# Semaphore waits on TensorE moved to earlier products, smaller fill products, another order at both ends of the kernel

## The chip, the cores and the metric

The kernel runs on one core of a Trainium2 chip. A core has five engines with a queue each: PE (TensorE, with its weight loads listed apart as PEld), DVE (VectorE), ACT (ScalarE), POOL (GpSimd) and SP (SyncE, which issues most of the DMAs here). They work side by side and wait for each other by semaphores. The metric is the time of the device for one execution, in microseconds (us); all times below are in us where nothing else stands.

## What is computed

Retention attention over 8 batches, 8 heads, 576 positions and heads of 64, then a mixture of small adapters on the result, in which each token takes 2 of 8 experts:

```python
scores = scale * np.matmul(q, k.transpose(0, 1, 3, 2))
Dmat = np.where(rel >= 0, gamma[:, None, None] ** rel[None, :, :], 0.0)
ret = np.matmul(scores * Dmat[None], v)              # B, H, S, D
x = ret.transpose(0, 2, 1, 3).reshape(B * S, H * D)  # 4608 x 512
logits = x @ w_gate
topk = np.argpartition(-logits, K, axis=1)[:, :K]    # K = 2
...                                                  # w: softmax of the two logits
delta[mask] += w[mask, k, None] * ((x[mask] @ A[e]) @ B[e])
return x + delta
```

## The kernel before, in words

**Units and rounds.** The 576 positions are cut into four chunks of 128 and a short one of 64. A unit is one chunk of two batches (or the short chunk of four); there are 16 full and 2 short units, `seq` lists them, and all four batch pairs of one chunk come before the next chunk. The short ones are units 14 and 17. The attention is done chunk by chunk with a running state `P` per batch pair, so the scores are needed only inside a chunk; units 0 to 3 (chunk 0) have no earlier state.

The loop over `t` from 2 to 17 is a software pipeline. Round `t` works on three units: `u` = t, `p1` = t-1 and `p2` = t-2. The program's order on every engine is that of the code, written out by hand (`tc.manual_schedule()`), and each engine runs its own queue in that order. In a full round PE does, in this order:

- `stage_B(p2)`: 8 transposes of x into the output bank (po), so that x is added to the adapters' result
- `stage_R0(p1)`: 16 products of masked scores with v, the same-half part, which finish px
- `stage_S(u)`: 32 products of q and k, the scores (ps)
- `stage_X(p2)`: two transposes of the routed z (pzt); `stage_Z(p1)`: 8 products of x with A and the gate (pz); `stage_Y(p2)`: 4 products with B (po)
- `stage_Q(u)`: 16 products of q with the state P (px); left out for chunk 0
- `stage_U(u)`: 16 products of v and k, the update of the state (pu)
- `stage_R1(u)`: 16 products of masked scores with v, the other part (px)
- `stage_T` for q and then k of unit t+1: 8 transposes each (pt_q, pt_k), 64 rows at a time

A product of float32 operands is two weight loads and two matmuls on PE, so the 32 products of the scores are listed as 64.

**The other engines.** DVE multiplies the transposed q by its decay out of PSUM (qT, two halves of a unit, line 254), masks the scores (rt, four per unit, line 306), adds to the state (pn, line 342) and does the routing: `route` finds the two best logits (max, ns), has ACT take the sigmoid (sg), and scales z (cm, zc). ACT copies the transposed k out of PSUM (kT, line 263): two copies per unit, r = 0 with the first 64 positions of every head pair and r = 1 with the second 64. In the scores, the products of the loop variable `late` = 0 read the first half of kT and those with `late` = 1 the second; the fifth product of `stage_S` is the first with `late` = 1. ACT also copies x (xT), the outputs (osb) and zT. POOL scales v by the decay (two halves, `scale_v`), swaps the halves of the second batch (vs) and decays the state. SP issues the loads of unit t+4 in round t, and the stores.

**Waits.** An instruction of an engine carries one wait on one semaphore. Where it has to wait for two, a record of its own stands ahead of it in the engine's queue and carries the other wait (EVENT_SEMAPHORE in the trace). In the kernel before a full round has five such records on PE: ahead of the first product of `stage_U` (which waits for DVE's masks, as its bank held scores, and for POOL's v), ahead of the first and the second transpose of q (its DMA, and DVE's routing, which read the bank before), ahead of the first transpose of k (its DMA and DVE), and ahead of the first product of `stage_S` (qT from DVE, kT from ACT).

**PSUM.** There are eight banks, k0 to k7, handed out by hand: `bank(i, ...)`. `a`, `c`, `d`, `e` in the loop name pairs of banks; `c` and `d` change places every round.

**Ahead of the loop.** PE first runs fill products on a constant tile `ones` while nothing else is there, then `pa`, which makes the table of decays `aqp`; units 0 and 1 run by hand-written order, with the making of the adapter weights AW (pl) between them.

**After the loop.** The last full unit (p1 = 16) and the last short one (u = 17) are routed, multiplied by B and stored.

Of the kernel before, what the change touches and what calls it, by code (L numbers as in the profile page):

```python
# [18 lines left out]
def kernel(  # L19
# [124 lines left out]
    seq.append((NFULL, 1))  # L144
    NU = len(seq)
    nat = {}


    def alloc_nat(i):
# [7 lines left out]
    def load_part(i, w):  # L157
        c, y = seq[i]
        src, tl = (q, k, v)[w], nat[i][w]
        for s in range(2):  # L160
            if c < NFULL:
                nc.sync.dma_start(  # L162
                    out=tl[:, s * H : s * H + H, :],
                    in_=src[2 * y + s, :, 128 * c : 128 * c + 128, :].rearrange(
                        "h j d -> j h d"
                    ),
                )
            else:
                b0, s0 = QUAD * y + 2 * s, 128 * NFULL
                nc.sync.dma_start(  # L170
                    out=tl[64 * s : 64 * s + LH, :, :],
                    in_=src[b0 : b0 + 2, :, s0 : s0 + LH, :].rearrange("b h j d -> j (b h) d"),
                )
# [17 lines left out]
        mybir.DependencyClass.Sync, mybir.DependencyReason.DATA  # L191
    )

    class Unit:
        pass

# [12 lines left out]
    flat = lambda t_: t_.rearrange("p a b d -> p (a b d)")  # L209

    def scale_b(u, b, eng):
        eng.tensor_tensor(  # L212
            out=u.v[:, b * H : b * H + H, :],
            in0=u.v[:, b * H : b * H + H, :],
            in1=(gv if u.full else gvh).unsqueeze(2).broadcast_to((128, H, Dh)),
            op=ALU.mult,
        )

    def swap_v(u):

# [11 lines left out]
    def stage_T(u, nm, bk, halves=False):  # L232
        src = u.q if nm == "q" else u.k
        dst = wk.tile([128, HP, 2, 128], FP32, tag=nm + "T", name=nm + "T", bufs=4)
        ps = [bank(bk[r], [128, HP, 2, 64], f"pt_{nm}") for r in range(2)]
        for b in range(2):
            for hp in range(HP):
                for r in range(2):
                    sl = slice(64 * r, 64 * r + 64)
                    nc.tensor.matmul(  # L240
                        ps[r][:, hp, b, :],
                        lhsT=src[sl, b * H + 2 * hp : b * H + 2 * hp + 2, :],
                        rhs=id64[sl, :],
                        is_transpose=True,
                        start=True,
                        stop=True,
                    )

        n = HP // 2 if halves else HP
        for hp in range(0, HP, n):  # L250
            for r in range(2):
                i_, hs = slice(64 * r, 64 * r + 64), slice(hp, hp + n)
                if nm == "q":
                    nc.vector.tensor_tensor(  # L254
                        out=dst[:, hs, :, i_],
                        in0=ps[r][:, hs],
                        in1=aqp[:, hs, i_ if u.full else slice(0, 64)]
                        .unsqueeze(2)
                        .broadcast_to((128, n, 2, 64)),
                        op=ALU.mult,  # L260
                    )
                else:
                    nc.scalar.copy(out=dst[:, hs, :, i_], in_=ps[r][:, hs])  # L263
        setattr(u, nm + "T", dst)

    def mm(o, l, r, start, stop):
# [33 lines left out]
    def mask(u, gs=(0, 1)):  # L300
        if 0 in gs:
            u.rt = [[None, None], [None, None]]
        for g in gs:
            for ho in range(2):
                r = wk.tile([128, 2, 3, 64], FP32, tag=f"rt{ho}", name=f"rt{ho}", bufs=4)
                nc.vector.tensor_tensor(  # L306
                    out=r.rearrange("p a s i -> p a (s i)"),
                    in0=u.ps[ho][g].rearrange("p a s i -> p a (s i)"),
                    in1=tri3.rearrange("p s i -> p (s i)").unsqueeze(1).broadcast_to((128, 2, 192)),
                    op=ALU.mult,  # L310
                )
                u.rt[ho][g] = r

    def stage_Q(u, bk):
        u.px = [bank(bk[b], [128, HP, 128], f"px{b}") for b in range(2)]
        if u.c == 0:
            return
        for hp in range(HP):
            for b in range(2):
                for ho in range(2):  # L320
                    mm(
                        u.px[b][half(ho ^ b), hp, :],
                        P[u.bp][half(ho), hp, b, :],
                        u.qT[half(ho), hp, b, :],
                        hp == 0,
                        False,
                    )

    def stage_U(u, bk):
        u.pu = bank(bk, [128, HP, 2, Dh], "pu")  # L330
# [13 lines left out]
            )  # L344
        nc.gpsimd.tensor_tensor(out=flat(P[u.bp]), in0=flat(pn), in1=flat(gdec), op=ALU.mult)  # L345

    def stage_R1(u):
        for b in range(2):
            for hp in range(HP):
                for ho in range(2):  # L350
                    mm(
                        u.px[b][half(ho ^ b), hp, 64:128],
                        u.vb[b][:, 2 * hp + ho, :],
                        u.rt[ho][hp // 2][:, hp % 2, 1 + b, :],
                        u.c == 0 and hp == 0,
                        True,
                    )

    def stage_R0(u, seen=None):
        first = True
        seen = seen or u.sum
        for hp in range(HP):
            for b in range(2):
                for ho in range(2):
# [7 lines left out]
                    if first:  # L374
                        tc.add_manual_dep(m.ins, seen.ins.name, done, reason="rows")
                        first = False


    def short_S(u, bk):
# [105 lines left out]

    def route(u, ss=(0, 1), away=False):
        if 0 in ss:
# [4 lines left out]
            u.zc = mo.tile([128, 2, ER], FP16, tag="zc", name="zc", bufs=4)  # L494
        m8, ns, sg, cm = u.rw
        z = {s: u.pz[s] for s in ss}
        if away:

            z[1] = mo.tile([128, ER + E], FP32, tag="z", name="z", bufs=1)
            nc.vector.tensor_copy(out=z[1], in_=u.pz[1])  # L500
        lg = {s: z[s][:, ER : ER + E] for s in ss}

        def best(s):
            nc.vector.max(out=m8[:, s, :], in_=lg[s])  # L504
            nc.vector.scalar_tensor_tensor(  # L505
                out=ns[:, s, :], in0=m8[:, s, 0:1], scalar=-1.0, in1=m8[:, s, 1:2],
                op0=ALU.mult, op1=ALU.subtract,
            )
            nc.scalar.activation(  # L509
                out=sg[:, s, :], in_=lg[s], func=AFT.Sigmoid, scale=2.0, bias=ns[:, s, :]  # L510
            )

        def times(s):
            nc.vector.scalar_tensor_tensor(
                out=cm[:, s, :], in0=lg[s], scalar=m8[:, s, 1:2], in1=sg[:, s, :],
                op0=ALU.is_ge, op1=ALU.mult,
            )
            nc.vector.tensor_tensor(
                out=u.zc[:, s, :].rearrange("p (e r) -> p e r", e=E),
                in0=z[s][:, 0:ER].rearrange("p (e r) -> p e r", e=E),  # L520
                in1=cm[:, s, :].unsqueeze(2).broadcast_to((128, E, R)),
                op=ALU.mult,
            )

        for s in ss:
            best(s)
        for s in ss:
            times(s)


    def stage_X(u, bk, cols=True):
# [69 lines left out]
    def filler(bk, n, cols):  # L601
        for _ in range(n):
            mm(
                bank(bk, [128, 4, 128], "fill")[:, 0 : cols // 128],
                ones[:, 0:128],
                ones[:, 0:128].unsqueeze(1).broadcast_to((128, cols // 128, 128)),
                True,
                True,
            )

    filler(7, 2, 512)
    pa = bank(6, [128, HP, 128], "pa")
    for hp in range(HP):
        mm(pa[:, hp, :], g8[:, 128 * (1 + hp) : 128 * (2 + hp)], g8[:, 0:128], hp == 0, True)
    nc.scalar.copy(out=aqp[:, 0 : HP // 2], in_=pa[:, 0 : HP // 2])
    nc.vector.tensor_copy(out=aqp[:, HP // 2 :], in_=pa[:, HP // 2 :])
    filler(7, 1, 256)
    for b in range(2):
        affine(tri3[half(b), 0 : 3 - b : 2 - b, :], [[0, 2], [1, 64]], -1, ALU.is_ge)
        nc.gpsimd.memset(tri3[half(b), 1 + b, :], 1.0)  # L620
# [22 lines left out]
    u0, u1 = get(0), get(1)  # L643
    stage_T(u0, "q", (2, 3), True)
    stage_T(u0, "k", (0, 1), True)
    filler(7, 1, 256)
    scale_b(u0, 0, nc.vector)
    scale_b(u0, 1, nc.gpsimd)
    swap_v(u0)
# [24 lines left out]
    stage_Z(u0, (2, 3))  # L674
    scale_v(u1)
    nc.gpsimd.dma_start(out=Bcat, in_=moe_B.rearrange("e r d -> (e r) d"))
    route(u0)
    stage_S(u1, (6, 7, 0, 1))
    mask(u1)
    stage_Q(u1, (6, 7))  # L680
    stage_U(u1, 4)
    state(u1)
    stage_R1(u1)
    transposes(2, (4, 5), (0, 1))

# [7 lines left out]
    for t in range(2, NU):  # L693
# [7 lines left out]
            stage_Z(p2, (None, c[0]), [1])  # L701
            route(p2, [1], True)
        if p1.full:
            stage_R0(p1)
            copy_x(p1)
            if u.full:
                stage_S(u, c + a)
# [15 lines left out]
        if u.full:  # L723
# [10 lines left out]
            else:  # L734
                stage_Q(u, c)
                stage_U(u, a[0])
                state(u)
                stage_R1(u)
        else:
            short_R(u)  # L740
            copy_x(u, True)
# [9 lines left out]
    stage_B(p1, a)  # L751
    stage_X(p1, d0, False)
    stage_Z(u, (d1, c[1]), [0])
    route(u, [0])
    stage_Z(u, (d1, c[1]), [1])
    stage_Y(p1)
    route(u, [1])
    evac(p1, [0])
    zT = mo.tile([128, 2, 128], FP16, tag="zT", name="zT")

    def last_X(s):
# [3 lines left out]
        )  # L765
        nc.scalar.copy(out=zT[:, s, :], in_=pzt)

    last_X(0)
    last_B(u, e + (c[0], d0))
    last_X(1)  # L770
    evac(p1, [1], nc.vector.tensor_copy)
    store(p1)
# [1 line left out]
    for s in range(2):  # L774
        for cc in range(2):
            mm(u.po[s][cc], zT[:, s, :], bv[:, :, cc ^ s, :], False, True)
        for cc in range(2):
# [3 lines left out]
            else:  # L781
                nc.scalar.copy(out=o, in_=u.po[s][cc])
        b0 = 4 * u.x + 2 * s
        nc.sync.dma_start(
            out=out3[b0 : b0 + 2, 128 * u.c : 128 * u.c + LH, :].rearrange("n t d -> t n d"),
            in_=u.osb[:, s].rearrange("p a o d -> p (a o d)"),
        )
# [31 lines left out]
```

## Time and profile before

| | us |
|---|---|
| median of 6 runs | 185.41 (182.98 to 187.21) |
| profiled execution, whole time | 182.98 |
| its span, first to last instruction | 181.3 |
| granted TensorE clock | 0.993 of full |
| DMA moved | 38.85 MB, 214 GB/s in the mean |

The profiled execution is one execution; its view of instructions is what the steps below are read from. Its page, cut down:

```profile
PE   7999899999999999999999999999998979999970
DVE  1546764745565756565555556565654663655560
ACT  3345154545353535353535344434341722335540
POOL 7470962918271809090908181727277007215000
DMA  6998999998999999998979998999999989511035
...
L254 DVE TENSOR_TENSOR qT<-pt_q,aqp 128x512 f32<-128x512 f32 (+1 forms) x38 | 23.3, 657 | 15.0 <-PE pt_q L240 15.0
L263 ACT COPY kT<-pt_k 128x512 f32<-128x512 f32 (+1 forms) x38 | 19.5, 568 | 31.4 <-PE pt_k L240 31.3
```

The first five rows cut the span into 40 equal slices of 4.5 us; a digit is the busy share of the slice in tenths. PE is full in nearly all of them and the DMA engines in most; the others are half busy. The last two rows are groups of instructions: line, engine, operation, what is written from what, shapes and count, then busy time and the mean of one in ns, then the idle time of the engine just ahead of them and what ended it. Both groups wait for PE: the queues of DVE and ACT are empty when the transposes come.

### The profile page before, as it was taken

The numbers are of one execution on the slowest core, as the hardware profiler recorded it, in microseconds if no ns is written. First come the engines' busy times: TensorE is split into PE (matmuls) and PEld (weight loads), VectorE is DVE, ScalarE is ACT, GpSimd is POOL, SyncE is SP. The second block draws the span as 40 slices with busy tenths as digits, with TensorE's granted clock in tenths as the row PEclk, the third lists the DMA queues.
The fourth block names the chain that finished last, engine by engine and source line by source line (L and its number), as shares of the span: only waits on it lengthen the run. The fifth ranks groups of instructions, "written<-read, shape, count | busy, mean of one in ns | idle before, by whom it ended". The sixth has DMA issues, their size and how long they took to land.

```text
span 181.3 us, 10252 instructions
## 1 busy us (share of the span) xinstructions
PE 171.8 (95%) x4636; PEld 155.2 (86%) x4636; DVE 100.6 (56%) x275; ACT 76.3 (42%) x177; POOL 81.4 (45%) x102
## 2 busy tenths in 40 slices
PE   7999899999999999999999999999998979999970
PEld 2789799999898989899999999999897969989850
DVE  1546764745565756565555556565654663655560
ACT  3345154545353535353535344434341722335540
POOL 7470962918271809090908181727277007215000
PEclk9999999999999999999999999999999999999997
DMA  6998999998999999998979998999999989511035
GB/s 139 263 221 201 233 230 229 227 232 199 248 260 222 254 217 264 218 259 187 277 174 289 245 264 185 247 214 247 218 264 222 276 185 281 205 56 66 4 124 225
DMA packets 119035, 38.85 MB, mean 214 GB/s; under 512 B 114248, under 2 KB 114376, under 8 KB 118992
## 3 DMA queue, kind: packets, MB, share of 16 engines
q1 hardware_dynamic: 118688, 38.04, 85.2%
q8 instruction: 36, 0.59, 1.3%
q0 software_dynamic: 144, 0.13, 0.6%
q10 hardware_dynamic: 160, 0.03, 0.1%
q14 instruction: 7, 0.06, 0.1%
HBM read 28.88 MB, written 9.44 MB: 211 GB/s over the span
## 4 chain that ended last, share of the span: by engine, by line
PE 87%; DVE 3%; DMA 2%; SPq 2%; issue 1%; POOL 1%; ACT 0%; ACTq 0%
PE px L267 23%; PE pz L267 19%; PE ps L267 11%; PE pu L267 9%; PE pt_q L240 6%; PE po L548 5%; PE pt_k L240 5%; PE po L267 4%; DMA v<-in_v_dram 2%; SPq L162 2%; PE pzt L536 2%; PE ps_s L267 1%; DVE rt L306 1%; DVE ns L505 1%; PE pl L267 1%
## 5 line engine op out<-in xcount | busy, mean ns | idle before, releaser
L345 POOL TENSOR_TENSOR P<-pn,gdec 128x512 f32<-128x512 f32 x16 | 20.4, 1275 | 72.9 <-DVE pn L342 54.0
L212 POOL TENSOR_TENSOR v<-v,pack 128x512 f32<-128x512 f32 x35 | 35.8, 1044 | 8.5 <-DMA v<-in_v_dram 8.5
L306 DVE TENSOR_TENSOR rt<-ps,tri 128x384 f32<-128x384 f32 x64 | 31.3, 550 | 14.5 <-PE ps L267 14.4
L267 PE MATMUL pz<-AW,xT 128*128 128x136 f32 x288 | 37.9, 284 | 0.7 <-issue 0.7
L267 PEld LDWEIGHTS pz<-AW,xT 128*128 128x128 f32 x288 | 34.7, 190 | 1.2 <-issue 0.9
L263 ACT COPY kT<-pt_k 128x512 f32<-128x512 f32 (+1 forms) x38 | 19.5, 568 | 31.4 <-PE pt_k L240 31.3
L254 DVE TENSOR_TENSOR qT<-pt_q,aqp 128x512 f32<-128x512 f32 (+1 forms) x38 | 23.3, 657 | 15.0 <-PE pt_q L240 15.0
L509 ACT ACTIVATE sg<-pz,ns 128x8 f32<-128x8 f32 x35 | 9.4, 268 | 42.0 <-PE po L267 26.5
L267 PE MATMUL ps<-qT,kT 64*64 64x128 f32 (+1 forms) x1024 | 25.9, 247 | 0.9 <-issue 0.9
L267 PEld LDWEIGHTS ps<-qT,kT 64*64 64x64 f32 x1024 | 23.8, 133 | 1.9 <-issue 1.1
L267 PE MATMUL px<-rt,v 64*64 64x64 f32 (+1 forms) x512 | 21.8, 224 | 0.2
L267 PE MATMUL px<-rt,vs 64*64 64x64 f32 (+1 forms) x512 | 21.2, 223 | 0.0
L223 POOL COPY vs<-v 64x512 f32<-64x512 f32 x32 | 19.5, 609 | 1.7
L267 PE MATMUL pu<-v,k 128*64 128x64 f32 x512 | 18.9, 225 | 0.7 <-POOL v L212 0.7
L267 PEld LDWEIGHTS px<-rt,v 64*64 64x64 f32 (+1 forms) x512 | 17.9, 136 | 1.9 <-DVE rt L306 0.4
L267 PEld LDWEIGHTS pu<-v,k 128*64 128x64 f32 x512 | 16.4, 137 | 3.6 <-issue 2.3
L450 ACT COPY xT<-px 128x512 f32<-128x512 f32 x33 | 18.0, 591 | 2.7 <-PE px L267 1.8
L504 DVE MAX8 m<-pz 128x8 f32<-128x8 f32 x35 | 6.1, 174 | 22.7 <-PE pz L267 16.5
L573 ACT COPY osb<-po 128x512 f32<-128x512 f32 x33 | 17.7, 588 | 0.0
L267 PEld LDWEIGHTS px<-rt,vs 64*64 64x64 f32 (+1 forms) x512 | 17.6, 136 | 0.0
L267 PE MATMUL px<-qT,P 64*64 64x128 f32 (+1 forms) x512 | 15.6, 262 | 0.0
L267 PEld LDWEIGHTS px<-qT,P 64*64 64x64 f32 x512 | 12.4, 133 | 2.6 <-DVE m L504 2.3
(68 smaller groups left out, 179.3 us busy)
## 6 DMA issues: line engine op xcount, KB each, us to landing
q<-in_q_dram SPq DMA_DIRECT2D x36, 256.0 KB, 5.0
k<-in_k_dram SPq DMA_DIRECT2D x36, 256.0 KB, 4.6
v<-in_v_dram SPq DMA_DIRECT2D x36, 256.0 KB, 4.6
out_dram<-osb SPq DMA_DIRECT2D x36, 256.0 KB, 4.3
A<-in_moe_A_dram SPq DMA_DIRECT2D x1, 256.0 KB, 4.1
Bcat<-in_moe_B_dram POOLq DMA_DIRECT2D x1, 128.0 KB, 3.7
g<-c_g ACTq DMA_DIRECT2D x1, 20.0 KB
pack<-c_rest ACTq DMA_DIRECT2D x1, 10.0 KB, 2.9
```

What stands on the lines that cost most here:

```text
L212: eng.tensor_tensor(out=u.v[:, b * H : b * H + H, :], in0=u.v[:, b * H : b * H + H, :], in1=(gv if u.full else gvh).unsqueeze(2).broadcast ...
L223: nc.gpsimd.tensor_copy(out=vs[half(1 - r)], in_=u.v[half(r), H : 2 * H, :])
L240: nc.tensor.matmul(ps[r][:, hp, b, :], lhsT=src[sl, b * H + 2 * hp : b * H + 2 * hp + 2, :], rhs=id64[sl, :], is_transpose=True, start=Tru ...
L254: nc.vector.tensor_tensor(out=dst[:, hs, :, i_], in0=ps[r][:, hs], in1=aqp[:, hs, i_ if u.full else slice(0, 64)] .unsqueeze(2) .broadcast ...
L263: nc.scalar.copy(out=dst[:, hs, :, i_], in_=ps[r][:, hs])
L267: return nc.tensor.matmul(o, lhsT=l, rhs=r, start=start, stop=stop, skip_group_check=True)
L306: nc.vector.tensor_tensor(out=r.rearrange("p a s i -> p a (s i)"), in0=u.ps[ho][g].rearrange("p a s i -> p a (s i)"), in1=tri3.rearrange(" ...
L345: nc.gpsimd.tensor_tensor(out=flat(P[u.bp]), in0=flat(pn), in1=flat(gdec), op=ALU.mult)
L450: nc.scalar.copy(out=o, in_=u.px[s])
L509: nc.scalar.activation(out=sg[:, s, :], in_=lg[s], func=AFT.Sigmoid, scale=2.0, bias=ns[:, s, :])
L548: nc.tensor.matmul(po[cc][:, s, dt, :], lhsT=u.xT[s][sl, dt, :], rhs=id64[sl, :], is_transpose=True, start=(dt == 0 and s == 0), stop=Fals ...
L573: copy(out=bass.AP(o.tensor, o.offset, ap), in_=u.po[cc])
```

## The change

It has five parts.

1. A helper `behind(m, other)` adds to a product a wait for an instruction of another engine. It is used at the end of three stages: the last two products of `stage_Q` wait for v's first scaling and for the last mask; the last three of `stage_R1` (in the loop, except where the unit ahead is short) wait for the routing of p1 and for the first loads of the next unit's q and k; the last one of `stage_R0` waits for the second kT copy of the unit whose scores come next. The products that follow then have one wait left each.
2. `route` is cut into `best` and `times`, so that the two can be issued apart.
3. The fill products at the start read 512 columns of `ones` in place of 128 repeated ones; one of 64 columns is added, two of 256 columns are taken out, and 13 products of 64 x 64 are put in ahead of unit 0's scores. The table `aqp` is made by one ACT copy in place of one half by ACT and one by DVE.
4. `route(u0)` is issued after `state(u1)` in place of ahead of `stage_S(u1)`.
5. At the end, both `best` are issued ahead of both `times`; the last transposes of x (`last_B`) come ahead of `last_X(0)`; the second of the last two stores is issued on ACT's queue in place of SP's.

The diff, without the lines that only keep the handles:

```diff
+    def behind(m, other):
+        tc.add_manual_dep(m.ins, other.ins.name, done, reason="split")
...
@@ def scale_b
+        if b == 0:
+            u.scaled = m
...
@@ def stage_T
-                    nc.scalar.copy(out=dst[:, hs, :, i_], in_=ps[r][:, hs])
+                    u.kT_made = nc.scalar.copy(out=dst[:, hs, :, i_], in_=ps[r][:, hs])
...
@@ def mask
-                nc.vector.tensor_tensor(
+                u.masked[g] = nc.vector.tensor_tensor(
...
@@ def stage_Q
+                    if hp == HP - 1 and b == 1:
+                        behind(m, (u.scaled, u.masked[1])[ho])
...
-    def stage_R1(u):
+    def stage_R1(u, ahead=()):
         for b in range(2):
             for hp in range(HP):
                 for ho in range(2):
...
+                    last = (b * HP + hp) * 2 + ho - 4 * HP + len(ahead)
+                    if last >= 0:
+                        behind(m, ahead[last])
...
-    def stage_R0(u, seen=None):
+    def stage_R0(u, nxt=None, seen=None):
...
+        if nxt:
+            behind(m, nxt.kT_made)
...
-    def route(u, ss=(0, 1), away=False):
+    def best(u, s, away=False):
...
+    def times(u, s):
...
+        u.routed = nc.vector.tensor_tensor(
...
+    def route(u, ss=(0, 1), away=False):
         for s in ss:
-            best(s)
+            best(u, s, away)
         for s in ss:
-            times(s)
+            times(u, s)
...
@@ def filler
-                bank(bk, [128, 4, 128], "fill")[:, 0 : cols // 128],
+                bank(bk, [128, 512], "fill")[:, 0:cols],
                 ones[:, 0:128],
-                ones[:, 0:128].unsqueeze(1).broadcast_to((128, cols // 128, 128)),
+                ones[:, 0:cols],
...
     filler(7, 2, 512)
+    filler(7, 1, 64)
...
-    nc.scalar.copy(out=aqp[:, 0 : HP // 2], in_=pa[:, 0 : HP // 2])
-    nc.vector.tensor_copy(out=aqp[:, HP // 2 :], in_=pa[:, HP // 2 :])
-    filler(7, 1, 256)
+    nc.scalar.copy(out=aqp, in_=pa)
...
     stage_T(u0, "k", (0, 1), True)
-    filler(7, 1, 256)
+
+    fb = [bank(i, [128, 64], "fill") for i in (7, 6)]
+    for i in range(13):
+        r, x = i % 2, i // 2 % 2
+        mm(fb[r ^ x][half(x), :], id64[half(r), :], id64[half(r), :], True, True)
...
-    route(u0)
     stage_S(u1, (6, 7, 0, 1))
     mask(u1)
     stage_Q(u1, (6, 7))
     stage_U(u1, 4)
     state(u1)
+    route(u0)
     stage_R1(u1)
...
-            stage_R0(p1)
+            stage_R0(p1, u)
...
-                stage_R1(u)
+                stage_R1(u, (p1.routed, landed[t + 1, 0, 0], landed[t + 1, 1, 0]))
...
     stage_Z(u, (d1, c[1]), [0])
-    route(u, [0])
+    best(u, 0)
     stage_Z(u, (d1, c[1]), [1])
+    best(u, 1)
+    times(u, 0)
+    times(u, 1)
     stage_Y(p1)
-    route(u, [1])
     evac(p1, [0])
...
+    last_B(u, e + (c[0], d0))
     last_X(0)
-    last_B(u, e + (c[0], d0))
     last_X(1)
...
-        nc.sync.dma_start(
+        (nc.sync, nc.scalar)[s].dma_start(
```

More of the change, by code (lines that the diff above doesn't have):

```diff
@@ L146 @@
     nat = {}
+    landed = {}
     def alloc_nat(i):
@@ L161, in load_part @@
             if c < NFULL:
-                nc.sync.dma_start(
+                landed[i, w, s] = nc.sync.dma_start(
                     out=tl[:, s * H : s * H + H, :],
@@ L169, in load_part @@
                 b0, s0 = QUAD * y + 2 * s, 128 * NFULL
-                nc.sync.dma_start(
+                landed[i, w, s] = nc.sync.dma_start(
                     out=tl[64 * s : 64 * s + LH, :, :],
@@ L211, in scale_b @@
     def scale_b(u, b, eng):
-        eng.tensor_tensor(
+        m = eng.tensor_tensor(
             out=u.v[:, b * H : b * H + H, :],
@@ L302, in mask @@
             u.rt = [[None, None], [None, None]]
+            u.masked = [None, None]
         for g in gs:
@@ L320, in stage_Q @@
                 for ho in range(2):
-                    mm(
+                    m = mm(
                         u.px[b][half(ho ^ b), hp, :],
@@ L350, in stage_R1 @@
                 for ho in range(2):
-                    mm(
+                    m = mm(
                         u.px[b][half(ho ^ b), hp, 64:128],
@@ L484, in last_B @@
                     )
-    def route(u, ss=(0, 1), away=False):
-        if 0 in ss:
+    def best(u, s, away=False):
+        if s == 0:
             u.rw = [
@@ L494, in route @@
             u.zc = mo.tile([128, 2, ER], FP16, tag="zc", name="zc", bufs=4)
+            u.z = {}
         m8, ns, sg, cm = u.rw
-        z = {s: u.pz[s] for s in ss}
+        u.z[s] = u.pz[s]
         if away:
[L499 to L523, printed above, removed]
+            u.z[s] = mo.tile([128, ER + E], FP32, tag="z", name="z", bufs=1)
@@ new lines, in best @@
+            nc.vector.tensor_copy(out=u.z[s], in_=u.pz[s])
+        lg = u.z[s][:, ER : ER + E]
+        nc.vector.max(out=m8[:, s, :], in_=lg)
+        nc.vector.scalar_tensor_tensor(
+            out=ns[:, s, :], in0=m8[:, s, 0:1], scalar=-1.0, in1=m8[:, s, 1:2],
+            op0=ALU.mult, op1=ALU.subtract,
+        )
+        nc.scalar.activation(
+            out=sg[:, s, :], in_=lg, func=AFT.Sigmoid, scale=2.0, bias=ns[:, s, :]
+        )
+    def times(u, s):
+        m8, ns, sg, cm = u.rw
+        nc.vector.scalar_tensor_tensor(
+            out=cm[:, s, :], in0=u.z[s][:, ER : ER + E], scalar=m8[:, s, 1:2],
+            in1=sg[:, s, :], op0=ALU.is_ge, op1=ALU.mult,
+        )
+        u.routed = nc.vector.tensor_tensor(
+            out=u.zc[:, s, :].rearrange("p (e r) -> p e r", e=E),
+            in0=u.z[s][:, 0:ER].rearrange("p (e r) -> p e r", e=E),
+            in1=cm[:, s, :].unsqueeze(2).broadcast_to((128, E, R)),
+            op=ALU.mult,
+        )
@@ L783 @@
         b0 = 4 * u.x + 2 * s
-        nc.sync.dma_start(
+        (nc.sync, nc.scalar)[s].dma_start(
             out=out3[b0 : b0 + 2, 128 * u.c : 128 * u.c + LH, :].rearrange("n t d -> t n d"),
```

## The prediction

> **What bounds the kernel now.** I read the page from its busy shares to its chain of waits. TensorE (PE) has work in 95% of the span and holds 87% of the chain; nothing else holds more than 3%.
>
> ```profile
> PE 171.8 (95%) x4636; PEld 155.2 (86%) x4636; DVE 100.6 (56%) x275; ACT 76.3 (42%) x177; POOL 81.4 (45%) x102
> PE 87%; DVE 3%; DMA 2%; SPq 2%; issue 1%; POOL 1%; ACT 0%; ACTq 0%
> ```
>
> The chain in order of time shows one stage of PE after another, and the same stage comes back after 9.29 us (scores ps at 69.98 and 79.28). So a round costs what its PE stages cost, and the question is what the change does inside them. The end of one round's transposes and the start of the next, in the chain:
>
> ```profile
> 67.70 0.64 PE pt_q L240 x16
> 68.34 0.51 PE pt_k L240 x16
> 68.85 0.51 PE po L548 x16
> 69.36 0.62 PE px L267 x32
> 69.98 1.40 PE ps L267 x64
> ```
>
> Each product is two weight loads and two matmuls here (float32), so x32 is the 16 products of stage_R0. Next the timeline of the same place, weight loads (PEld) and ACT:
>
> ```profile
> 68.12 0.59 PEld L240 LDWEIGHTS pt_k<-id,k 64*128 64x128 f32 x16
> 68.89 1.07 ACT L263 COPY kT<-pt_k 128x512 f32<-128x512 f32 x2 [2.21 <-PE pt_k L240]
> 69.63 0.14 PEld L267 LDWEIGHTS px<-rt,v 64*64 64x64 f32 x2
> 69.64 0.14 PEld L267 LDWEIGHTS px<-rt,vs 64*64 64x64 f32 x2
> ...
> 69.78 0.17 PEld L267 LDWEIGHTS ps<-qT,kT 64*64 64x64 f32 x3
> 70.01 0.22 PEld L267 LDWEIGHTS ps<-qT,kT 64*64 64x64 f32 x7
> ```
>
> This is the pair that decides. The second kT copy ends at 68.89 + 1.07 = 69.96. The scores start at 69.78 because their first four products need only the first copy; the fifth product needs the second half, and its first load is at 70.01, 0.05 after the copy. Down the trace that distance is 0.05 in rounds 2 to 14, all but one of them (round 6, 0.17). The copies always end 1.34 to 1.39 after the last pt_k load starts, whatever PE does between. So the scores already lean on the second copy, with four products of cover.
>
> [...] about 0.21 from the last load of a stage to the first of the next wherever the shape changes (R1 to pt_q 67.42 to 67.63; po to px 69.08 to 69.29), and the second has no wait record. Those gaps are therefore not the records' and stay. [...] the records (EVENT_SEMAPHORE, 51 ns each) ahead of pt_q stand at 76.27 and 76.39, while pt_q's first load is at 76.92. [...] a waiting product holds all behind it, and the 0.05 above shows that.
>
> **Part 1: five records fewer.** In the kernel before, a full round has five records on PE: ahead of U (waits DVE), of pt_q's first and second product, of pt_k, and of the scores S. As work that is 5 x 0.051 = 0.26 a round, but four run 0.4 to 0.75 us before the product they guard, while PE works: they cost 0. The one ahead of S (69.706 to 69.757, released by qT's end at 69.67) moves S from 69.75 to 69.78; that 0.03 lies under the kT wait. If all were on the path the gain would be 14 x 0.26 = 3.6; I take 0.
>
> **Part 2: the waits in their new places.**
> - Last two products of Q: wait for v scaled (POOL, 69.98) and the last mask (DVE, 72.73); they run at 74.7. Free. Behind them stands U, which needs both anyway.
> - Last three products of R1: wait for route (DVE) and for q and k of the next unit. Those loads landed 10 us or more earlier in the steady rounds and at least 1.7 us earlier in rounds 2 and 3: free. Route ends at 66.75, R1's third last product is at 67.3: free from round 4 on. In rounds 2 and 3 there is no Q and PE is ahead:
>
> ```profile
> 30.64 0.29 DVE L518 TENSOR_TENSOR zc<-pz,cm 128x128 f16<-128x128 f32 x1
> 30.80 0.82 PEld L240 LDWEIGHTS pt_q<-id,q 64*128 64x128 f32 x16
> ```
>
>  Route ends at 30.93. Now only pt_q's second product waits for it (pt_q takes 0.82, not the 0.58 of later rounds). After, R1 stands from 30.4 to 30.98, then runs its last 7 loads (0.2), [...] and pt_q starts near 31.36 and lasts 0.44 to its last load: 31.80 against 31.48. Some +0.3, twice: +0.6.
> - Last product of R0: waits for the second kT copy. This is the dear one. Its first load was at 69.65 (the last of the row at 69.64); now it cannot come before 69.96 + 0.05 = 70.01. Behind it: the second pass of R0's last four products (0.058 each four), then S, whose own first four products need 0.176 from first load to the fifth product's. So the fifth score product is at 70.01 + 0.058 + 0.038 + 0.176 = 70.28 instead of 70.01: **+0.27 a round**. Four products of S that used to cover the wait now stand behind it. Nothing gives it back: ACT's xT copies, DVE's masks and pz all follow PE, and the kT copies follow pt_k. Full rounds with it: 2 to 13, twelve (in round 16 the copy is 1 us early): 12 x 0.27 = +3.2. In the two short rounds (14, 17) the third score product already waits; +0.11 each, +0.2. Bounds: 0.15 a round if the loads held back come in a burst and S's own pause goes, 0.40 if the wait also breaks R0's four-product order.
>
> **Part 3: head.** The fills now read 512 columns of ones, so they wait for the second memset (0.4 later), one small fill is added, two of 256 columns go, 13 of 64 x 64 come; aqp is one ACT copy (0.59 by the copies of that shape) instead of ACT then DVE. All of it lies before this:
>
> ```profile
> 9.17 1.04 POOL L212 TENSOR_TENSOR v<-v,pack 128x512 f32<-128x512 f32 x1 [2.52 <-DMA v<-in_v_dram]
> 10.27 0.90 PEld L267 LDWEIGHTS pu<-v,k 128*64 128x64 f32 x28 [0.38 <-POOL v L212]
> ```
>
>  PE waits at 10.27 for v, which waited for its DMA; the issue order on SP is untouched. 0, between -0.2 and +0.5[...]. route(u0) moved behind state(u1) frees the masks of unit 1, which waited behind it from about 18.4, when half of S was done, to 19.70: R1 could end 0.7 sooner. But pt_k of unit 2 needs k, whose second half lands at 23.24, and pt_k ends at 23.48 now: the gain ends in that DMA wait. 0. route then ends near 22.9, before po needs its bank at 23.54.
>
> **Part 4: tail.**
>
> ```profile
> 173.63 0.29 DVE L518 TENSOR_TENSOR zc<-pz,cm 128x128 f16<-128x128 f32 x1
> 173.84 0.16 DVE L504 MAX8 m<-pz 128x8 f32<-128x8 f32 x1
> ...
> 174.85 0.29 DVE L518 TENSOR_TENSOR zc<-pz,cm 128x128 f16<-128x128 f32 x1
> 176.73 1.21 SPq L784 DMA_DIRECT2D out_dram<-osb  x2
> ```
>
>  The second max now comes ahead of the first cm and zc, so the last zc ends about 0.19 sooner; the first zc ends 0.5 later, which the transposes moved ahead (last_B) fill. The last two stores leave SP one after the other, 0.66 apart; the second goes to ACT's queue, behind ACT's own copies (176.48). [...] Last landing 179.74 becomes about 179.1: -0.6, between 0 and -0.9.
>
> **Sum:** +3.2 + 0.6 + 0.2 + 0 - 0.6 = +3.4. The profiled execution took 182.98 (span 181.3 and 1.7 around it); it is the fastest of the six, 2.4 below their median 185.41. So 186.4 on its scale (span near 184.7), **188.8** as a median.
>
> **The rivals.**
> - *The records are on the path and the kT wait is not (faster).* For it: [...] the waits view shows 0.17 ahead of U in 13 rounds. Against it: the gaps without records are as long. Price: -3.6 - 0.6 gives 181.2; it decides if a record costs more than the 0.27 / 5 = 0.054 that the R0 wait gives back. 15%.
> - *The held loads come in a burst (no change).* 12 x 0.10 + 0.3 - 0.6 = +0.9, 186.3. DMA, busy in nine tenths of most slices, gains slack. 17%.
> - *The wait breaks R0's order of passes (slower still).* 12 x 0.40 + 0.8 - 0.3 = +5.3, 190.7. 13%.
> - Forecast as worked out: 55%. That the five records don't go is unlikely: each new wait is on the same engine's counter as the one it replaces, or on the same load.
>
> **The numbers.** 1% is 1.85 us, about what a measurement can tell from no change. Slower by over 1% (above 187.3): forecast and third rival nearly whole, 0.65. Within 1%: the second rival and the forecast's lower edge, 0.20. Faster: 0.15. The range reaches down to 184.0 (partial mixes of the first two rivals) and up to 190.6.
>
> **What would show it.** PE's instruction count of records down by some 70; the load of the last px<-rt,vs 0.05 behind kT's end in every round, S starting about 0.1 after that, a round of 9.56; pt_q of rounds 2 and 3 near 0.58 long but later; last two stores issued within 0.2 of each other. Wrong if the round stays at 9.29 or falls.

## The result and the profile after

The changed kernel takes **187.01 us** (median of 20 runs, 185.28 to 189.18) against 185.44 for the kernel before in the same session (41 runs). The ratio is **1.0152 [1.0123, 1.0182]**, that is +2.8 us. Ratios here compare the executions within 1.5% of each kernel's fastest, so they need not equal the ratio of the medians (+1.6 us). The profiled execution took 185.7, its span is 184.0 at a clock of 0.996: 2.7 longer than the one before.

The page of the changed kernel: busy time by engine, then the shares of the chain of waits.

```profile
PE 174.9 (95%) x4660; PEld 156.9 (85%) x4660; DVE 99.4 (54%) x274; ACT 76.5 (42%) x177; POOL 81.7 (44%) x102
...
PE 80%; SPq 9%; DVE 3%; DMA 2%; issue 2%; ACT 1%; ACTq 0%
```

PE is still what bounds it, now with 3.1 us more of "work". (SPq holds 9% instead of 2% because the chain now begins with SyncE's issuing of loads, up to the k of unit 2.) The chain in order of time (start, length, stage) shows where the work is:

```profile
79.59 0.51 PE pt_k L248 x16
80.10 0.51 PE po L565 x16
80.61 0.62 PE px L275 x30
81.26 0.27 PE px L275
81.53 1.40 PE ps L275 x41
```

R0 no longer runs through: 30 of its 32 matmuls, then a late piece, and only then the scores. The timeline one round earlier, weight loads and ACT:

```profile
70.55 1.07 ACT L271 COPY kT<-pt_k 128x512 f32<-128x512 f32 x2 [2.21 <-PE pt_k L248]
...
71.56 0.24 PEld L275 LDWEIGHTS px<-rt,vs 64*64 64x64 f32 x3
71.68 0.15 PEld L275 LDWEIGHTS ps<-qT,kT 64*64 64x64 f32 x3
71.73 0.13 PEld L275 LDWEIGHTS px<-rt,vs 64*64 64x64 f32 x1
```

The second kT copy ends at 71.62. The third of the three px loads is R0's last product; it starts at 71.674, 0.05 after the copy, and the scores' first load follows at 71.68. In the kernel before that first load was 0.18 *ahead* of the copy's end. The distance is 0.05 in eleven of the twelve rounds 2 to 13 (round 6: 0.10, with a pause of PE in it that comes up below), and from end of copy to end of copy an undisturbed round is **9.587** where it was 9.293. In the waits view (what waited for what: us in total, times, longest) these are new:

```profile
PEld px L275 <- ACT kT L271: 2.1, 12, 0.2
...
PEld px L275 <- DVE zc L534: 0.7, 2, 0.4
```

The 2.1 is not the whole price. It counts the idle time ahead of the last product, not the four score products that used to run in it. The second line is R1's wait for the routing in rounds 2 and 3, here in the timeline of round 2:

```profile
30.61 0.29 DVE L534 TENSOR_TENSOR zc<-pz,cm 128x128 f16<-128x128 f32 x1
...
30.96 0.31 PEld L275 LDWEIGHTS px<-rt,vs 128*64 128x64 f32 x6 [0.37 <-DVE zc L534]
31.33 0.58 PEld L248 LDWEIGHTS pt_q<-id,q 64*128 64x128 f32 x16
```

R1's last six loads stand until zc's end; pt_q starts late and then runs in 0.58 instead of 0.82. These two rounds are 0.68 and 0.63 longer, of which 0.29 each is R0's. Last the tail, in the timeline:

```profile
177.42 0.29 DVE L534 TENSOR_TENSOR zc<-pz,cm 128x128 f16<-128x128 f32 x1
...
179.29 0.55 SPq L806 DMA_DIRECT2D out_dram<-osb  x1
179.29 0.65 ACTq L806 DMA_DIRECT2D out_dram<-osb  x1
```

Counted from the start of the last Z stage, the last zc ends 0.3 sooner than before and the last store is issued 0.98 sooner, side by side with the other; yet the span's end comes only 0.16 sooner (9.77 after the Z stage, 9.93 before).

So twelve rounds lost 0.294 each (+3.5), rounds 2 and 3 another 0.73, and the tail (what follows the start of the last Z stage) won 0.16. That is more than the +2.7 between the two spans. Most of the rest was won in rounds 14 to 16, where the kernel before has two pauses of PE, 0.97 and 1.16 long (from the start of one record to the start of the next), that the profile puts down to "issue", and the changed kernel has smaller ones. The experiments had two questions: is the R0 wait the cause, and what are these pauses.

### The profile page after: what moved, and what is told of

Same layout as the page of the kernel before. It is cut to its first block, busy times and chain, and to the rows that moved or that the text cites. A ratio compares the mean times of both kernels' runs of the same rounds, so it can differ in the third digit from the quotient of the medians.

```text
span 184.0 us, 10237 instructions
## 1 busy us (share of the span) xinstructions
PE 174.9 (95%) x4660; PEld 156.9 (85%) x4660; DVE 99.4 (54%) x274; ACT 76.5 (42%) x177; POOL 81.7 (44%) x102
## 4 chain that ended last, share of the span: by engine, by line
PE 80%; SPq 9%; DVE 3%; DMA 2%; issue 2%; ACT 1%; ACTq 0%
PE px L275 23%; PE pz L275 18%; PE ps L275 11%; SPq L163 8%; PE pu L275 7%; PE pt_q L248 5%; PE po L565 5%; PE pt_k L248 4%; PE po L275 4%; DMA k<-in_k_dram 2%; PE pzt L553 2%; PE ps_s L275 1%; DVE zc L534 1%; SPq L126 1%; ACT sg L524 1%
## 5 line engine op out<-in xcount | busy, mean ns | idle before, releaser
L275 PE MATMUL ps<-qT,kT 64*64 64x128 f32 (+1 forms) x1024 | 26.9, 247 | 0.2 <-issue 0.2
L275 PE MATMUL px<-rt,vs 64*64 64x64 f32 (+1 forms) x512 | 26.1, 225 | 0.9 <-DVE zc L534 0.5
L275 PEld LDWEIGHTS ps<-qT,kT 64*64 64x64 f32 x1024 | 24.6, 133 | 0.9 <-issue 0.3
L275 PEld LDWEIGHTS px<-rt,vs 64*64 64x64 f32 (+1 forms) x512 | 20.4, 136 | 2.9 <-ACT kT L271 2.1
```

The lines of the kernel that those rows point to most:

```text
L275: return nc.tensor.matmul(o, lhsT=l, rhs=r, start=start, stop=stop, skip_group_check=True)
```

## Experiments

**The parts of the waits.** Four kernels, compared with a kernel before of 186.75. First the changed kernel without the R0 wait:

```
-            stage_R0(p1, u)
+            stage_R0(p1)
```

> The changed kernel with one wait taken back: the last product of R0 no longer waits for the second kT copy (a full round has one record again, ahead of S; 40 on PE in all instead of 27). Theory 1, that this wait costs 0.29 in twelve rounds and 0.1 in the two short ones: 3.7 us less than the changed kernel, 183.3 beside 187.0, ratio to the kernel before about 0.99 to 1.00; the fifth score product loads 0.05 behind the kT copy again and a round from 4 on is 9.29. Theory 2, that the loss is made by the waits at the end of R1 (route and the next unit's loads) or by the two ends: within 1 us of the changed kernel, ratio about 1.015, rounds stay at 9.59.

The R0 wait put alone into the kernel before:

```
-                    nc.scalar.copy(out=dst[:, hs, :, i_], in_=ps[r][:, hs])
+                    u.kT_made = nc.scalar.copy(out=dst[:, hs, :, i_], in_=ps[r][:, hs])
...
+        if nxt:
+            behind(m, nxt.kT_made)
...
-            stage_R0(p1)
+            stage_R0(p1, u)
```

> The kernel before with only the wait of R0's last product for the second kT copy (13 records fewer on PE, all else as before). Theory 1: the loss is made by this wait alone: +3.7 us on 185.4, ratio about 1.020, rounds of 9.59 from round 4 on. Theory 2: ratio 0.997 to 1.003, rounds of 9.29. If records are worth 0.05 each on the path, it would be 0.7 less than theory 1 says, ratio 1.016.

Here is the end of R0 in that kernel; the second kT copy ends at 81.88, and the scores again come behind it:

```profile
80.81 1.07 ACT L266 COPY kT<-pt_k 128x512 f32<-128x512 f32 x2 [2.21 <-PE pt_k L243]
...
81.94 0.13 PEld L270 LDWEIGHTS px<-rt,vs 64*64 64x64 f32 x1 [0.17 <-ACT kT L266]
81.95 0.15 PEld L270 LDWEIGHTS ps<-qT,kT 64*64 64x64 f32 x3
```

The changed kernel with R0's last product waiting for the *first* kT copy:

```
-                    u.kT_made = nc.scalar.copy(out=dst[:, hs, :, i_], in_=ps[r][:, hs])
+                    made = nc.scalar.copy(out=dst[:, hs, :, i_], in_=ps[r][:, hs])
+                    if r == 0:
+                        u.kT_made = made
```

> The changed kernel with R0's last product waiting for the first kT copy in place of the second; the records stay away (27 on PE). The first copy ends 0.18 before that product would load, so theory 1 expects no stall there: 3.7 us less than the changed kernel, ratio 0.99 to 1.00, and within 0.3 us of the run without the R0 wait, since the record ahead of S that it saves moves S by 0.03 only and the kT wait of the fifth product covers that. If records do lie on the path, it is 0.7 us or more faster than the run without the R0 wait (14 records of 0.05).

And the same without the routing wait where a unit has no Q (rounds 2 and 3):

```
-                stage_R1(u, (p1.routed, landed[t + 1, 0, 0], landed[t + 1, 1, 0]))
+                stage_R1(u, (p1.routed, landed[t + 1, 0, 0], landed[t + 1, 1, 0])[u.c == 0 :])
```

> As the run with the first kT copy, and in the rounds of chunk 0 (2 and 3) the end of R1 no longer waits for the routing; from round 4 on it does. Theory 1: rounds 2 and 3 get back 0.35 each, 0.7 us less than the run with the first copy, ratio to the kernel before about 0.99 to 0.995. If the routing wait in these rounds is hidden: no difference to that run.

| kernel | undisturbed round | rounds 2, 3 | ratio to before |
|---|---|---|---|
| before | 9.293 | 8.47, 8.49 | 1 |
| changed | 9.587 | 9.15, 9.12 | 1.0152 |
| without the R0 wait | 9.293 | 9.21, 8.82 | 0.9935 [0.9899, 0.9971] |
| R0 wait alone | 9.59 | 8.78, 8.77 | 1.0085 [1.0038, 1.0132] |
| first copy | 9.273 | 8.80, 8.80 | 0.9875 [0.9735, 1.0015] |
| first copy, no early routing wait | 9.273 | 8.56, 8.46 | 0.9861 [0.9772, 0.9951] |

The round settles the first question: the wait alone makes it 9.59, its absence 9.293, whichever kernel it is in. Without the routing wait rounds 2 and 3 fell by 0.24 and 0.34, where 0.35 was expected of each; the times of the last two kernels can't tell that apart. Without the R0 wait the timeline has the scores following R0 again, ahead of the copy's end at 71.56:

```profile
70.48 1.08 ACT L271 COPY kT<-pt_k 128x512 f32<-128x512 f32 x2 [2.21 <-PE pt_k L248]
...
71.30 0.14 PEld L275 LDWEIGHTS px<-rt,vs 64*64 64x64 f32 x2
71.38 1.01 PEld L275 LDWEIGHTS ps<-qT,kT 64*64 64x64 f32 x44
```

It also shows what four records fewer in a round are worth on the path: nothing, 9.293 as before. The fifth, ahead of the scores, was worth 0.020 (9.273 with the first copy; R0's last product then carries that wait, and the record ahead of S is gone). But the *times* do not add up: the R0 wait alone should have cost 3.5 (1.019) and cost 1.6, and the kernel without it is faster than the kernel before, though its rounds 2 and 3 are slower. So the wait is shown as the cause of the longer round, while the ratio of the times holds something else as well.

**Dose, records, stores, and one thing better.** Compared with a kernel before of 188.21. The wait on R0's first product instead of its last:

```
                     if first:
                         tc.add_manual_dep(m.ins, seen.ins.name, done, reason="rows")
+                        if nxt:
+                            behind(m, nxt.kT_made)
```

> The kernel before, with the wait on the second kT copy put on the FIRST product of R0 instead of the last (nothing else changed). Theory 1 (a wait costs what the products behind it take, up to the fifth score product): all of R0's loads, which took 0.36 from first to last ahead of the copy's end, now come behind it, on top of the 0.294 that the last product's wait cost: a round of 9.293 + 0.29 + 0.36 = 9.94, 12 rounds x 0.65 = +7.8 us, ratio near 1.042. Theory 2 (a wait on a product of R0 costs a fixed pause of some 0.3, wherever it stands): a round of 9.59, +3.5 us, ratio 1.009 to 1.02.

The round became **9.96**, ratio 1.0315 [1.0229, 1.0401]. The timeline:

```profile
73.65 0.14 PEld L270 LDWEIGHTS px<-rt,v 64*64 64x64 f32 x2 [0.79 <-ACT kT L266]
...
74.11 0.21 PEld L270 LDWEIGHTS ps<-qT,kT 64*64 64x64 f32 x8
```

All of R0 stands behind the copy's end (73.60), 0.46 to the first score. The wait costs what stands behind it: 0.29 with one product of R0, 0.67 with sixteen. The ratio, here too, lies below the sum of the rounds (1.042 by theory 1) and above what theory 2 allows.

The waits split over Q and R1 put into the kernel before, with no R0 wait and the old head and tail (46 records fewer):

```
+                    if hp == HP - 1 and b == 1:
+                        behind(m, (u.scaled, u.masked[1])[ho])
...
+                    last = (b * HP + hp) * 2 + ho - 4 * HP + len(ahead)
+                    if last >= 0:
+                        behind(m, ahead[last])
```

> The kernel before, with the waits split over the last two products of Q and the last two or three of R1 (without the route wait where a unit has no Q), but without the R0 wait, the head, and the tail: some 46 records fewer on PE. Theory 1 (records run ahead of the products they guard, and cost nothing; the free waits stay free): a round of 9.29, ratio 0.997 to 1.003. Theory 2 (records are on the path at 0.051 each): a round of 9.09, ratio 0.985 to 0.99.

The undisturbed rounds are 9.293, as theory 1 has it, but the ratio is 0.9868 [0.9817, 0.9918], as theory 2 has it. Neither expectation held whole.

The last store alone on ACT's queue:

```
-        nc.sync.dma_start(
+        (nc.sync, nc.scalar)[s].dma_start(
```

> The kernel before, with only the last store issued on ACT's queue instead of SP's. Theory 1 (both leave together but [...] land later: 2.4 and 3.0 after issue): from the last Z stage to the end 9.6 to 9.8 instead of 9.925, the time unchanged within 0.3 us. Theory 2 (the prediction's: the 0.66 of later issue is all gained): from the last Z stage to the end 9.3, the last store landing within 2.4 of its issue.

Ratio 1.0000 [0.9964, 1.0036], and 10.0 from the last Z stage to the end (of its profiled execution, a long one of 192.6 us, only this tail is read). First the two stores of this kernel in the trace, then those of the kernel before; the last line of each gives the least, median and most time from issue to landing:

```profile
L784 SPq DMA_DIRECT2D out_dram<-osb x1: 551/551/551, 186.3 to 186.3; - x1
L784 ACTq DMA_DIRECT2D out_dram<-osb x1: 662/662/662, 186.3 to 186.3; - x1
...
DMA to landing us min/median/max: 2.4/2.7/3.0
```

```profile
L784 SPq DMA_DIRECT2D out_dram<-osb x2: 545/548/550, 176.7 to 177.4; - x2
...
DMA to landing us min/median/max: 2.3/2.3/2.3
```

Issued together, the stores land 2.4 and 3.0 after their issue. One after the other on SP's queue, the second lands 2.3 after its own (the trace doesn't tell the landing of the first). What is issued 0.66 sooner thus takes 0.7 longer. So the other queue alone gained nothing, and the 0.16 of the changed tail must have come with the earlier zc and last_B, which were not tried alone.

Last, on top of the kernel with the first copy and no early routing wait, the scores in another order, so that eight products instead of four precede the first that reads the second kT copy:

```
-            for a in range(2):
-                hp = 2 * g + a
-                for late in range(2):
+            for late in range(2):
+                for a in range(2):
+                    hp = 2 * g + a
```

> The kernel with the wait of R0 on the first kT copy and no route wait in rounds 2 and 3, in which S now takes its products of each mask group by the half of kT: the first eight read only the first copy (four before). Theory 1 (S waits for the second copy at its fifth product, with about 0.05 to 0.07 a round left of that wait): the ninth product is issued after the copy has ended, the wait goes, a round of 9.20 to 9.23 instead of 9.273, and 0.5 to 0.9 us less; faster than both kernels, ratio near 0.98 against the kernel before. Theory 2 (TensorE had work queued over that wait, so it costs nothing): a round of 9.27, the same time[...].

The round is **9.233** (9.273 without), so PE did stand 0.04 at that wait. Ratio 0.985 [0.9802, 0.9897]: faster than the kernel before, and, if one divides the two ratios of different sessions, 3% under the changed one. Its gain over the order before it, 0.04 a round, is below what the times can tell.

**The pauses.** One DMA queue that the profile calls "instruction" moved 36 packets of 16,384 bytes in the kernel before. Each packet is one entry in the trace's list of DMA packets; the page has their sum (packets, MB, share of the 16 DMA engines):

```profile
q8 instruction: 36, 0.59, 1.3%
```

PE has 9,363 records in the kernel before (9,350 in the changed one, also with 36 packets), 260 a packet. That these packets bring PE's instructions is inferred from this and from what follows. I numbered PE's records (loads, matmuls, waits, drains) in order of their start and looked where the pauses over 0.3 us without a named cause stand:

| kernel | pauses, sum | record number modulo 256 | end, after the last packet's end |
|---|---|---|---|
| before | 2, 2.1 us | 193 | 1.46, 1.52 |
| changed | 4, 1.6 us | 193 | 1.40 to 1.52 |
| first copy | 4, 2.8 us | 193 | 1.16 to 1.50 |
| R0 wait alone | 5, 3.1 us | 193 | 1.24 to 1.54 |
| records alone | 6, 4.1 us | 193 | 1.34 to 1.63 |

The ten traces so far agree, and they suggest that a pause comes where one block of 256 instructions ends and the next came late. (Why the remainder is 193 and not 0 the traces don't show.) The next experiment moves only the blocks: 136 instructions more in the head of the kernel before.

```
-    filler(7, 1, 256)
+    shift(18)
```

Here `shift(n)` runs n of the changed kernel's 64 x 64 fill products; both fills of 256 columns are replaced.

> The kernel before, with its two fill products of 256 columns in the head replaced by 36 of 64 x 64: 136 instructions more on TensorE, all in the head, nothing changed in the rounds. Theory F (the pauses that the profile calls issue come where TensorE's instructions pass from one block of 256 to the next and the next 16 KB packet on the instruction queue isn't there yet; in the traces so far they stand at record 193 modulo 256 and end some 1.4 after that packet's end): the blocks now end in other stages of the round. With the delays of the packets seen in ten traces, the sum of expected pauses goes from 4.7 to about 7.6 us: +2 to +3.5 us, ratio 1.01 to 1.02, with the pauses again at 193 modulo 256 of the records, and in other stages. Rival theory (the pauses have nothing to do with the place in the program): 36 small products cost their own 0.3 to 0.8 in the head at most, and the pauses stand in the same stages as before.

Ratio **1.0353 [1.0271, 1.0435]**, medians 195.33 against 187.81: +6.6 to +7.5 us for work that costs 0.4 in the head (end of the first kT copies 9.14, before 8.72). Undisturbed rounds are still 9.293. The profile has 11 such pauses, 11.9 us, all at 193 modulo 256 although the program around them has moved by 136. Before and shifted kernel in the waits view:

```profile
PEld ps L267 <- issue: 1.1, 1, 1.1
...
PEld pz L267 <- issue: 0.9, 1, 0.9
```

```profile
PEld ps L267 <- issue: 6.6, 6, 1.6
...
PEld po L548 <- issue: 1.9, 1, 1.9
```

and one of them in the shifted kernel's timeline, in the middle of the scores, where nothing but "issue" is named:

```profile
105.48 0.57 PEld L267 LDWEIGHTS ps<-qT,kT 64*64 64x64 f32 x22
107.67 0.75 PEld L267 LDWEIGHTS ps<-qT,kT 64*64 64x64 f32 x29 [1.62 <-issue]
```

Theory F holds in mechanism; its size, +2 to +3.5 us by the packet delays pooled over the ten traces, was too small by half or more.

Then three kernels in which the loads of units 6 to 17 are left out, those units taking the data of the unit six earlier:

```
     def load(i):
+        if i >= 6:
+            nat[i] = nat[i - 6]
+            return
```

> The kernel before, with the loads of units 6 to 17 left out (they take the q, k and v of the unit six earlier; the stores stay). Theory F (late instruction packets queue behind the loads): packets start earlier, no pause at a block's end; rounds 9.29 throughout, time near 181, that is the profiled 181.3 less its pauses of 2.1 plus 1.7, and little spread between runs. Rival theory (pauses are TensorE's own, or of the clock): the time stays within 1 us of the kernel before's median, pauses as before.

> The changed kernel with the same loads left out. Theory F (the sum of the prediction is right for a TensorE that is never short of instructions, and part of the loss is won back by fewer pauses): against the same cut of the kernel before, +2.8 to +3.5 us, near 184. Rival theory (the waits cost less than the sum says, or something else won time back): +1.2 to +2 us as with the loads, near 182.7.

> The kernel before with the records of Q and R1 gone (the split waits alone, no R0 wait, same head and tail), which was 1.6 us faster than before with all loads, here with the loads of units 6 to 17 left out. Theory F (the records themselves cost nothing; what was won lies in pauses): the same time as the kernel before cut alike, within 0.4 us. Rival theory (each record costs something on the path): 1.2 to 2.4 us faster than it.

Against the full kernel before: 0.9712 [0.9644, 0.9780] for before cut, 0.9876 [0.9824, 0.9927] for the changed kernel cut, 0.9662 [0.9613, 0.9711] for the records cut; medians 182.77, 184.96, 181.17. Waits view of the changed kernel cut:

```profile
PEld px L279 <- ACT kT L275: 2.4, 14, 0.2
PEld pu L279 <- issue: 2.3, 13, 0.2
```

The R0 wait stands; of the pauses none over 0.3 is left. In the kernel before cut there are three, where theory F had none: two in rounds 4 and 5, at 45 and 55 us (the last of the loads that are left lands at 51.9), and one in round 17. From round 7 to 13 every round of the three is 9.293 or 9.587. There the packets also come sooner: between 70 and 130 us they start 0.2 to 0.3 us (medians of the three traces) after PE has passed into a block, against 0.8 to 2.2 in the eleven traces with all loads. So without most of the loads the kernel before wins 5 us (182.77 where 181 was expected). Fewer late instruction packets are part of it; other waits for loads went too, and the two were not told apart. The difference changed minus before is +3.1 by the ratios, as theory F has it, and +2.2 by the medians, between the two theories. The records cut are 0.9 to 1.6 faster than before cut, so that theory F's "within 0.4" failed in the time, while the undisturbed rounds are equal; in the two profiled executions the difference stands in the head, ahead of unit 2's kT copies (1.4), and at pauses and disturbed rounds (1.6).

## Why the prediction was right, and where it was off

The forecast was 188.8, slower by over 1%; it came to 187.0, ratio 1.0152 (by the medians alone, 0.8%).

- **R0 wait, +0.27 a round, twelve rounds: right in mechanism and place, a little small.** 0.294, so +3.5 for +3.2. All three signs came: 0.05 behind the copy, S behind it (0.06, 0.1 said), a round of 9.587 for 9.56. The dose test shows that the price is the products held back (0.29 with one of R0 behind the wait, 0.67 with sixteen). The rival in which the held loads come in a burst (0.15 in one place of the prediction, 0.10 in another), and the one in which R0's order of passes breaks (0.40), are out.
- **Records, 0: right for the round.** Four of five cost nothing, the fifth 0.020 instead of "lies under the kT wait". The rival with the records on the path fails at the round of 9.293. PE's records fell by 61 (88 to 27), not by 70.
- **Routing wait in rounds 2 and 3, +0.6:** 0.39 and 0.34, +0.73.
- **Short rounds, +0.2:** the one at t = 14 lost 0.11 as said (8.51 for 8.39 in the kernels without most loads); that at t = 17 has a pause of 0.35 in it and can't be read.
- **Head, 0:** the gain of unit 1 ended, as said, in the wait for unit 2's k, whose landing differs by 0.3 between the two executions anyway.
- **Tail, -0.6: this is the term that was mis-sized.** The stores did leave together, but the step took the landing time of a single store. That nearly all of the 0.66 of later issue would be won was the author's estimate; with the store on ACT's queue alone the two landed 2.4 and 3.0 after their issue instead of 2.3, and nothing was won. -0.16 in its place.
- **What the prediction did not have: the instruction packets.** The steps above sum to +4.2, more than the +3.4 of the forecast and the 2.7 between the two spans. The prediction says nothing of the pauses of 2.1 us in rounds 14 and 15 of the kernel before, and its profiled execution was the fastest of six, 2.4 under the median. How far pauses differ between the executions of one kernel was not traced. A kernel with other instructions has its blocks end elsewhere: 529 PE records a round before, 524 after. What they did between the two profiled executions can be read by laying PE's products beside the same products of the kernels without most loads. In rounds 14 to 16 the kernel before lost 2.4 us, the changed one 0.9, and in both each step of over 0.1 by which PE falls behind begins within a few records of a block's end; some are shorter than 0.3. That gave back 1.5. Unit 2's k, which landed 0.3 sooner, gave another 0.3, and rounds 5 and 6, disturbed in the kernel before, 0.2; round 17, with its pause and its R0 wait, took 0.5. So 4.2 became 2.7.
- **That +3.4 lies as near to +2.8 as it does is in part luck.** The R0 term was too small a loss and the tail too large a gain, 0.7 together; what the late blocks gave back, which no term of the sum foresaw, hid that. How much of the difference of the medians the late blocks make was not measured, and it stays open why the kernel with records alone is 1.3% faster than before; its gain is not in the undisturbed rounds.

The range, 184.0 to 190.6, held it with room.

## What to carry to other kernels

A wait moved to an earlier product freed no time here by removing a record that ran ahead of its product (a round of 9.293 with four fewer, as with all five); ask instead which products stood between the old place and the new one, for they now stand behind the wait. If a wait must be carried by an earlier instruction, give it the part of the other engine's work that the next stage needs first (here the first copy), and let the products that need the rest come last. Where one engine runs a long program while the DMA engines are busy in nine tenths of most slices, as here, look for "issue" pauses at equal distances in the program (here multiples of 256 records) before explaining a difference of a few us by the edit.

## What the runs showed of the hardware

- The traces agree with instructions of PE that come in blocks of 256, one to a packet, and with a PE that stops for a late block: in fourteen traces 62 pauses over 0.3 us stand at record 193 modulo 256 and end 1.16 to 1.63 (median 1.39) after the last packet's end. The same holds where no pause is seen: number the packets from 0, and in none of 491 places does PE pass record 193 + 256 (n + 1) sooner than 1.11 after the end of packet n. Between 26 us and the last Z stage only two other pauses (0.42 and 1.07) are called issue; both end 0.07 after a small ACT copy (`see`) that their product waits for. The pauses at 193 sum to 1.6 to 11.9 us in the eleven kernels with all loads, of 181 to 193 us.
- A packet starts 0.2 to 2.3 us after PE has passed into a block (the middle 80% of the traces), takes 0.96 (median), and the pauses end some 1.4 after it: at the late end that is 4.7. A block lasts 3.6 to 5.5 us in the full rounds of the kernel before, so there is no slack where it is short.
- Two stores of 256 KB issued at once from SP and ACT landed after 2.4 and 3.0 us (one trace); the second of two issued 0.66 apart from SP landed after 2.3.
- In the traces of the kernel before and after, none of the 9,995 and 10,042 instructions of the engines carries more than one wait, the records (EVENT_SEMAPHORE) not counted. PE has 88 records before and 27 after, 51 ns each in the median; five and three of them carry two waits.
- Between 66 and 95 us of the kernel before, 0.20 to 0.31 pass from the last load of a stage to the first of the next at the five places of a round where the loads' shape changes, and at most 0.13 between other loads. No run tested whether the change of shape is the cause.
